# A decode step of attention and an MLP: the output weight loaded in four pieces instead of five, its columns split 320 to 256, and the last wait moved to GpSimd

## The chip, the cores and the metric

The kernel runs on one core of one Trainium2 chip. Its time is device microseconds of one execution, told as a median over several. The page and the views of the profile come from one profiled execution, which has a time of its own.

## What is computed

A batch of four rows, one token each, width 576. The input is normalised once; an attention over the last 2048 places of a cache (32 query heads, 16 heads of K and V) and an MLP block run on it, and the results are added to the input:

```python
def _A_ref(x, k_cache, v_cache, wq, wo):                 # x: 4 x 1 x 576
    q = (x @ wq).reshape(B, Sq, Hq, Dh)...               # 32 heads of 128
    scores = einsum("bhqd,bhkd->bhqk", q, k[last 2048]) * Dh**-0.5
    o = einsum("bhqk,bhkd->bhqd", softmax(scores), v[last 2048])
    return o.reshape(B, Sq, Hq * Dh) @ wo                # wo: 4096 x 576
def _B_ref(x, w1, w2, w3, w4):
    h = gelu(layernorm(x) @ w1)                          # one token: half of its shifted groups are zeros
    x1 = x + shifted(h) @ w2
    return x1 + gelu(layernorm(x1) @ w3) @ w4            # w4: 4608 x 576
xn = layernorm(x)
return x + _A_ref(xn, ...) + _B_ref(xn, ...)
```

All inputs and the output are bf16. The weights and the parts of the caches that are read come to 88.5 MB.

## The kernel before

The program is written engine by engine. Each operation is put on a list of its engine with what it waits for and a key; every list is sorted by key (L613) and issued in that order. Nothing else decides the order of the work.

**The stream of loads.** All loads but that of the input go through SP's queue in the order of their keys: w1, w2, wq, w3, then sixteen chunks of K (2 MB each), eight of V (4 MB each, the last one in two halves), w4 and wo. A load waits until the buffer it overwrites has been read: the chunks of K for the transposes of an earlier chunk, those of V for the products of an earlier chunk. w4 (L273) waits until the sixth chunk of V has been used; wo comes behind it in the queue, in pieces (L295 to L299).

**The middle.** TensorE transposes K in blocks of 128 (L485), VectorE and ScalarE copy the blocks out (L469, L468), TensorE takes the scores (L492); softmax, a transposition of the probabilities (L514, L520), then the products with V (L553) while the chunks of V land. A fold (L559, L571 to L577) brings the two heads of a group apart, and three more steps (L580 to L583) make ORT, the attention's output, with the 4096 inner values laid over 128 partitions and 32 rows.

**The end.** The output has 4 rows of 576 columns. It is added up in two accumulators of 288 columns each (`ACC`, L161), which lie in different 32-row groups of the accumulation memory. `pe_t1` (L585) puts input plus MLP residual into them, `pe_MO` (L455) adds w4's product, 36 rows of 128 inner values, two matmuls a row, one for each half of the columns; then wo's product follows, 32 rows, again two matmuls a row (L596 to L607). Ahead of w4's product stand eight matmuls on zeros (`pe_idle`, L592). wo is cut by `WO_ROWS` (L20) into pieces of 13, 10, 5, 3 and 1 rows, each a load with a semaphore of its own; the product of a piece waits for its piece alone. A row of wo is 128 partitions of 576 values, 144 KB. Every piece waits on SP for the same uses of V as before the change, and all of them stand behind w4.

In the last piece the half of columns 288 to 575 goes first (`for h in (1, 0)`, with a smaller key for it). When a half's last matmul is done, VectorE copies columns 288 to 575 (L609) and ScalarE columns 0 to 287 (L608) into `out_sb`. The output's load to memory is issued by ScalarE when both are done (L300), and SP waits for it to land (L301); this is the last instruction of the program.

The lines that the prediction's steps touch: L20, L161, L199 (where every load is issued), L273, L295 to L301, L392 (the helper `acc_mm`, where w4's and wo's matmuls are recorded), L449 and L526 (other evictions), L460, L553, L588, L592, L596 to L609.

Of the kernel before, what the change touches and what calls it, by code (L numbers as in the profile page):

```python
# [7 lines left out]
ACTF = mybir.ActivationFunctionType  # L8
# [8 lines left out]
NVS = 4  # L17
NPAIR = 2
ACT_EVAC = (1, 4, 7)
WO_ROWS = (13, 10, 5, 3, 1)  # L20
WOA = 28
V_IDLE = 4
O_IDLE = 8
# [14 lines left out]
def bass_parallel_sum__sliding_block_cached__mixer_s_mlp__decode_kernel(  # L38
    nc, A_x, A_k_cache, A_v_cache, A_wq, A_wo, B_x, B_w1, B_w2, B_w3, B_w4, out
):  # L40
    B, Sq, D = A_x.shape
# [14 lines left out]
    scale = float(Dh) ** -0.5  # L56
    EPS = 1e-5
    HALF = D // 2
    FH = F // 2
    W4R = F // 128  # L60
    CH = [(b, gq) for gq in range(4) for b in range(B)]
# [8 lines left out]
    with ExitStack() as ctx:  # L70
        def sb(name, shape, dt):
            return ctx.enter_context(nc.sbuf_tensor(name, shape, dt))
# [16 lines left out]
        wq_t = kring[:, 2 * UE:2 * UE + 9 * NQ // 2]  # L89
        w3_t = vring[:, 0:9 * FH]  # L90
        w4_t = vring[:, 5 * UE - W4R * D:5 * UE].rearrange("p (r n) -> p r n", r=W4R)
        assert 9 * FH <= 4 * UE
        assert WOA * D <= 2 * UE and (32 - WOA) * D + W4R * D <= 3 * UE
        wo_at = lambda a: a * D if a < WOA else 2 * UE + (a - WOA) * D
        wot = lambda a, n: vring[:, wo_at(a):wo_at(a) + n * D].rearrange("p (r n) -> p r n", r=n)
        _o = 0

        def cut(n):
            nonlocal _o
            _o += n  # L100
            return ktb[:, _o - n:_o]
        w1_t = cut(9 * HALF)
        w2_t = cut(9 * HALF)
        assert _o <= NKT // 2 * 1024
# [18 lines left out]
        hs_inT = sb("hs_inT", [128, 9, 2, B], BF16)  # L123
        hh_sb = sb("hh_sb", [2 * B, HALF], BF16)
        h2_sb = sb("h2_sb", [128, 64 * 9], BF16)
        q_sb = vring[:, 5 * UE - 512:5 * UE]
        h2T_sb = sb("h2T_sb", [128, W4R, B], BF16)
# [6 lines left out]
        ident_f = sb("ident_f", [128, 128], FP32)  # L134
# [16 lines left out]
        ORT = sb("ORT", [128, 32, B], BF16)  # L151
        t1 = sb("t1", [B, D], FP32)
        out_sb = sb("out_sb", [B, D], BF16)

        ps = ctx.enter_context(nc.psum_tensor("ps", [128, 8, 512], FP32))[:]
# [2 lines left out]
        OTps = ps[:, 1, 0:2 * NX]  # L158
        rinvps = ps[:, 5, 0:128]
        ORps = ps[:, 2, 0:128]  # L160
        ACC = [ps[32 * k:32 * k + B, 7, 0:HALF] for k in range(2)]  # L161
        Qps = ps[:, 4, :]
        QTps = ps[:, 0, 0:256].bitcast(BF16).rearrange("p (n j x) -> p n j x", n=4, j=4)
        HSps = ps[0:B, 5, 0:HALF]
        HHps = ps[0:2 * B, 3, 0:HALF]
        TS = ((0, 5), (5, 4))
# [4 lines left out]
        S = {}  # L171
# [16 lines left out]
        def add(engine, emit, waits=(), sig=None, key=0.0, inc=None):  # L188
            seqc[0] += 1
            prog[engine].append(Op(emit, waits, sig, key, seqc[0], inc))  # L190

        def add_dma(pairs, skey, waits=(), key=0.0, engine="sp"):
            if skey not in S:
                S[skey] = sem("s_" + "_".join(str(k) for k in (skey if isinstance(skey, tuple) else (skey,))))
            dma_count[skey] = dma_count.get(skey, 0) + 16 * len(pairs)

            def emit(e):
                for o_, i_ in pairs:
                    e.dma_start(o_, i_).then_inc(S[skey], 16)  # L199
            add(engine, emit, waits, None, key)  # L200
            return ("dma", skey, dma_count[skey])
# [21 lines left out]
        KE = KV + 40.0  # L223
# [26 lines left out]
        for gl in range(2):  # L250
            for x in range(2 * NVS):
# [3 lines left out]
                  waits=["pick11"], sig=f"pick2{gl}{x}", key=-84 + 0.1 * (8 * gl + x))  # L255


        def mask_of(t, tag, view):
            add("dve", lambda e: e.tensor_reduce(out=t[:], in_=view, axis=AX.X, op=ALU.add), waits=["ident_f"], sig=tag, key=-8)
        add("dve", lambda e: e.tensor_reduce(out=par[:], in_=ident_f[:].rearrange("p (m a) -> p a m", a=2), axis=AX.X, op=ALU.add),  # L260
            waits=["ident_f"], sig="par", key=-29.5)
# [32 lines left out]
        ev_wo, WOR, a = [], [], 0  # L294
        for n, rc in enumerate(WO_ROWS):  # L295
            ev_wo.append(add_dma([(wot(a, rc), wos[:, a:a + rc, :])], ("wo", n), [f"PV{2 * (NCV - NVS + (a >= WOA)) + 1}"], KS + NC + n))
# [1 line left out]
            a += rc  # L298
        assert a == 32  # L299
        ev_o = add_dma([(o2, out_sb[:])], "out", ["fin1", "fin0"], 10000, engine="act")  # L300
        add("sp", lambda e: e.wait_ge(S[ev_o[1]], ev_o[2]), (), None, 10001)  # L301


        def ln_ops(idx, src, dst, first_waits, tag, k0):
# [79 lines left out]
        for k in range(2):  # L384
            for g in range(2):
                add("dve", lambda e, k=k, g=g: e.tensor_copy(
                        out=qp_out[:, :, 2 * k + g].rearrange("p b (j n) y -> p b j n y", j=2),
                        in_=QTps[:, :, 2 * g:2 * g + 2, B * k:B * (k + 1)].rearrange("p (n y) j b -> p b j n y", y=2)),
                    waits=["qTp"] + (["qpad_zero"] if k + g == 0 else []), sig=f"qT{2 * k + g}", key=-10 + 0.1 * k)

        def acc_mm(e, h, lhsT, rhs, start=False, stop=False):
            return e.matmul(ACC[h], lhsT=lhsT, rhs=rhs, start=start, stop=stop, tile_position=(0, 32 * h), skip_group_check=True)  # L392

# [14 lines left out]
        for h in range(2):  # L408
# [3 lines left out]
                waits=[f"hs{h}"], sig="x1" if h else "x1a", key=-27 + 0.1 * h)  # L412
# [3 lines left out]
            waits=["hT", "ln3_sd"], sig="gelu_h", key=-25.9)  # L416
# [5 lines left out]
        def pe_h2(k):  # L422
            t0, n = TS[k]

            def f(e):
                ins = None
                for s_ in range(9):
                    w = w3_t[:, FH * s_:FH * (s_ + 1)].rearrange("x (p t) -> x p t", t=W4R)
                    for j in range(4):
# [17 lines left out]
        for k in range(2):  # L447
            add("pe", pe_h2(k), waits=[ev_w3] + (["xs20", "xs21", "gelu_h", "h2_zero"] if k == 0 else []), sig=f"h2_{k}", key=-18 + k)
            add("act", lambda e, k=k: e.activation(out=h2_v[k], in_=H2ps[k], func=ACTF.Gelu_apprx_tanh), waits=[f"h2_{k}"],  # L449
                sig=f"gelu2_{k}", key=-5 + 0.1 * k)  # L450
# [4 lines left out]
        def pe_MO(t0, t1):  # L455
            def f(e):
                ins = None
                for t in range(t0, t1):
                    for h in range(2):
                        ins = acc_mm(e, h, h2T_sb[:, t, :], w4_t[:, t, HALF * h:HALF * (h + 1)])  # L460
                return ins
            return f
        add("pe", lambda e: e.wait_ge(S["pool"], resolve("perm_bf")[1]), waits=["qT3"], key=-1)
# [2 lines left out]
        def evac(n):  # L466
            if n % 8 in ACT_EVAC:
                return "act", lambda e: e.activation(out=ktbuf[:, n % NKT], in_=tb[n % 4], func=ACTF.Copy)  # L468
            return "dve", lambda e: e.tensor_copy(out=ktbuf[:, n % NKT], in_=tb[n % 4])  # L469

        for n in range(NB):
            c, k = n // NBLK, n % NBLK
            if k == 0:
                add("dve", lambda e, c=c: e.tensor_copy(out=Qs[:, c % N_CB, :], in_=Qpad_t[:, 128 * (4 * CH[c][0] + CH[c][1]):][:, 0:128]),
                    waits=[f"SC{c - 2}"] if c >= 1 else ["qT3"], key=n)
            eng, f = evac(n)
            w = [f"T{n}"] + ([f"SC{c - 2}"] if c >= 1 else [])
            add(eng, f, waits=w + (["hT", "hs1", "h2_1"] if n == 0 else []), key=n + 0.2, inc=(("E", n % LB), 1))
# [9 lines left out]
        def emit_SC(e, k):  # L488
# [11 lines left out]
            waits=["rmax"], sig="negb", key=KS + 0.05)  # L500
        for q in range(4):
            add("act", lambda e, q=q: e.activation(out=P_sb[:, q, :], in_=Sps[:, q, :], func=ACTF.Exp,
                                                   bias=negb[:, 0:1], scale=scale, accum_out=rs4[:, q:q + 1]),
                waits=["negb"], sig=f"exp{q}", key=KS + 0.1 + 0.01 * q)
# [16 lines left out]
        for qt in range(4):  # L521
            k0 = KS + 0.9 + 0.1 * qt
            add("pe2", pe_PT(qt), waits=[f"PTx{q}" for q in range(4)] + (["pick217"] + [f"E{NB - 1 - k}" for k in range(4)] if qt == 0 else []),
                sig=f"PTp{qt}", key=k0)
            if qt % 2 == 1:
                add("dve", lambda e, qt=qt: e.tensor_copy(out=PT_t[:, 512 * qt:512 * (qt + 1)], in_=ps[:, 4 + qt, :]),  # L526
                    waits=[f"PTp{qt}"], sig=f"PT{qt}", key=k0)
            else:
                add("act", lambda e, qt=qt: e.activation(out=PT_t[:, 512 * qt:512 * (qt + 1)], in_=ps[:, 4 + qt, :], func=ACTF.Copy),
                    waits=[f"PTp{qt}"], sig=f"PT{qt}", key=k0)  # L530
# [3 lines left out]
            waits=["rinv", "ident_f"], sig="diag", key=KS + 0.82)  # L534
        add("pe2", lambda e: e.matmul(rinvps, lhsT=ones_f[:], rhs=diag[:], start=True, stop=True),
            waits=["diag", "ones_f", "PT1"], sig="rinvp", key=KV + 0.5)
        add("dve", lambda e: e.tensor_copy(out=rinvB[:].rearrange("p (c u e) -> p c u e", u=NU, e=2),
                                           in_=rinvps.rearrange("p (u c e) -> p c u e", u=NU, e=2)),
            waits=["rinvp"], sig="rinvB", key=KV - 2)
# [29 lines left out]
        for bp in range(NPAIR):  # L569
            k0 = KV + 2 * NVS * (bp + 1) - 0.5  # L570
            add("dve", lambda e: e.tensor_scalar(out=tmp[:], in0=ps[:, 0, 128:256], scalar1=maskd[:, 1:2], scalar2=None, op0=ALU.mult),  # L571
                waits=[f"PV{2 * NVS * (bp + 1) - 1}", "maskd"], sig=f"F{bp}", key=k0)
# [4 lines left out]
                waits=["rinvB", f"fold{bp}"], sig=f"O{bp}", key=k0 + (3 if bp == 0 else 0.2))  # L577
# [5 lines left out]
            waits=["OR"], sig="ORT", key=KE + 0.3)  # L583

        def pe_t1(e):  # L585
            ins = None
            for h in range(2):
                ins = e.matmul(ACC[h], lhsT=ident_f[0:B, 0:B], rhs=t1[:, HALF * h:HALF * (h + 1)], start=True, stop=False,  # L588
                               tile_position=(0, 32 * h), skip_group_check=True)
            return ins  # L590
        add("pe3", pe_t1, waits=["t1", "ident_f", "PT3"], sig="t1in", key=KE - 4)
        add("pe3", pe_idle(O_IDLE), key=KE + 0.25)  # L592

        add("pe3", pe_MO(0, W4R), waits=[ev_w4, "h2T"], key=KE + 10)
        last_p = len(WOR) - 1
        for n, (r0, r1) in enumerate(WOR):  # L596
            def f(e, r0=r0, r1=r1, hs=(0, 1)):
                ins = None
                for r in range(r0, r1):
                    for h in hs:  # L600
                        ins = acc_mm(e, h, ORT[:, r, :], wot(r, 1)[:, 0, HALF * h:HALF * (h + 1)], stop=(r == 31))
                return ins
            if n < last_p:
                add("pe3", f, waits=[ev_wo[n], "ORT"], sig=f"AO{n}", key=KE + 20 + n)
            else:
                for h in (1, 0):
                    add("pe3", lambda e, f=f, h=h: f(e, hs=(h,)), waits=[ev_wo[n]], sig=f"AOl{h}", key=KE + 20 + n - 0.1 * h)  # L607
        add("act", lambda e: e.activation(out=out_sb[:, 0:HALF], in_=ACC[0], func=ACTF.Copy), waits=["AOl0"], sig="fin0", key=KE + 50)  # L608
        add("dve", lambda e: e.tensor_copy(out=out_sb[:, HALF:D], in_=ACC[1]), waits=["AOl1"], sig="fin1", key=KE + 50)  # L609


        for eng in prog:
# [38 lines left out]
        e = nc.tensor  # L651
        emit_program("pe", "pe", e)
        with nc.Fori(0, N_LOOP, engines=[PE]) as it:
# [7 lines left out]
            for j in range(LB):  # L661
                emit_T(e, j, wait)
                if j % NBLK == 2:
                    k = (j // NBLK - 1) % N_CB
# [53 lines left out]
```

## Time and profile before

| | us |
|---|---|
| median of 3 runs | 214.08 (213.81 to 214.11) |
| the profiled execution | 213.93 |
| its span, first to last instruction | 212.6 |
| mean granted TensorE clock in it | 0.928 |
| PE busy in it (81% of the span) | 172.5 |
| DVE busy in it (53%) | 111.9 |
| ACT busy in it (28%) | 58.6 |
| bytes loaded, and their mean rate | 88.49 MB, 416 GB/s |
| the share of SP's queue of the 16 DMA engines' time | 97.7% |

The engines' names in the profile: PE is the matmul side of TensorE and PEld its loading of weights, DVE is VectorE, ACT is ScalarE, POOL is GpSimd, and SPq or ACTq is the issuing side of an engine. In the row of slices each digit is a fortieth of the span in tenths of busy time; PEclk is the granted TensorE clock, in tenths of full speed. In the timeline a row gives start, length, engine, line, operation, what it writes and reads, the count of instructions that were merged into it and, in brackets, how long the engine had been idle ahead of it and what released it. A matmul's end is modelled, and matmuls overlap, so a merged row's length is from its first start to its last end.

### The profile page before, as it was taken

Reading aid. Unit: us, or ns where it says so; the run is one execution under the profiler, and the core shown is the slowest. Engines: PE = TensorE matmul, PEld = TensorE weight load, DVE = VectorE, ACT = ScalarE, POOL = GpSimd, SP = SyncE. Lnnn points to the kernel's source line nnn. Section 1 sums busy time; section 2 is a strip of 40 time slices with the busy share of each in tenths; the row PEclk is TensorE's granted clock in tenths of the full one; section 3 lists DMA queues with packets and bytes.
Section 4 is the critical chain, followed back from the end, with each engine's and each line's share of the span. In section 5 each row is a group of like instructions: output and inputs, shape, how many; then the busy total and the mean of one; then the engine's idle time right before and its main releaser. Section 6 shows DMA issues by size and latency. Waiting matters only on the chain.

```text
span 212.6 us, 4856 instructions
## 1 busy us (share of the span) xinstructions
PE 172.5 (81%) x2212; PEld 133.7 (63%) x2216; DVE 111.9 (53%) x168; ACT 58.6 (28%) x69; POOL 15.6 (7%) x38
## 2 busy tenths in 40 slices
PE   1456147999999999999996089999989598997495
PEld 0222014888878888887774048988868487883262
DVE  5433200477776777777764869995575444003000
ACT  2004001366665566666656520000000000000000
POOL 8991000000000000000000000000000000000000
PEclk9997855899999999999999589999999889999799
DMA  6999999999999999999999999999999999999993
GB/s 242 453 444 445 429 396 416 432 425 427 429 416 438 432 422 429 435 422 424 432 444 438 444 407 459 413 425 453 407 444 438 419 425 410 451 476 393 407 408 131
DMA packets 5066, 88.65 MB, mean 417 GB/s; under 512 B 568, under 2 KB 704, under 8 KB 1216
## 3 DMA queue, kind: packets, MB, share of 16 engines
q1 hardware_dynamic: 5040, 88.49, 97.7%
q8 instruction: 8, 0.13, 0.3%
q14 instruction: 2, 0.02, 0.0%
q10 hardware_dynamic: 16, 0.01, 0.0%
HBM read 88.49 MB, written 0.00 MB: 416 GB/s over the span
## 4 chain that ended last, share of the span: by engine, by line
DMA 47%; PE 45%; DVE 4%; SPq 1%; ACT 1%; issue 1%
PE ps L485 23%; DMA vring<-in_A_wo_dram 15%; DMA vring<-in_B_w_dram 13%; DMA vring<-in_A_v_cache_dram 12%; PE ps L553 11%; DMA kring<-in_A_k_cache_dram 7%; PE ps L492 6%; PE ps L430 2%; SPq L199 1%; DVE vring L520 1%; DVE rmax L498 1%; DVE ktb L545 1%; PE ps L514 1%; PE ps L347 1%; ACT ktb L468 0%
## 5 line engine op out<-in xcount | busy, mean ns | idle before, releaser
L469 DVE COPY ktb<-ps 128x1024 bf16<-128x1024 bf16 x80 | 53.8, 689 | 23.5 <-PE ps L485 23.4
L485 PEld LDWEIGHTS ps<-perm_bf,kring 128*128 128x128 bf16 x1024 | 58.2, 98 | 8.3 <-issue 7.6
L485 PE MATMUL ps<-perm_bf,kring 128*128 128x128 bf16 x1024 | 61.7, 220 | 0.2
L468 ACT ACTIVATE ktb<-ps 128x1024 bf16<-128x1024 bf16 x48 | 48.0, 1023 | 32.5 <-PE ps L485 32.1
L545 DVE TENSOR_TENSOR ktb<-kring,mH_bf 128x4096 bf16<-128x4096 bf16 x16 | 36.2, 2286 | 14.6 <-PE ps L553 14.6
L553 PE MATMUL ps<-vring,ktb 128*128 128x256 bf16 x256 | 30.3, 282 | 4.3 <-DMA vring<-in_A_v_cache_dram 3.5
L553 PEld LDWEIGHTS ps<-vring,ktb 128*128 128x128 bf16 x256 | 25.7, 101 | 8.5 <-issue 3.6
L553 PE MATMUL ps<-kring,ktb 128*128 128x256 bf16 x256 | 28.6, 273 | 0.9 <-DMA kring<-in_A_v_cache_dram 0.9
L553 PEld LDWEIGHTS ps<-kring,ktb 128*128 128x128 bf16 x256 | 25.0, 98 | 4.5 <-issue 1.1
L608 ACT ACTIVATE out_sb<-ps 4x288 bf16<-4x288 f32 x1 | 0.4, 399 | 84.6 <-PE ps L392 84.6
L492 PE MATMUL ps<-ktb,Qs 128*32 128x512 bf16 x272 | 17.8, 382 | 1.2 <-ACT ktb L468 1.2
L430 PE MATMUL ps<-vring,xs 128*8 128x320 bf16 (+1 forms) x72 | 4.5, 429 | 7.6 <-DMA vring<-in_B_w_dram 7.6
L492 PEld LDWEIGHTS ps<-ktb,Qs 128*32 128x32 bf16 x272 | 5.7, 96 | 6.7 <-DVE ktb L469 1.4
L514 PE MATMUL ps<-vring,pick_bf 128*32 128x256 bf16 x64 | 3.9, 411 | 6.4 <-DVE rinv L532 6.4
L609 DVE CAST out_sb<-ps 4x288 bf16<-4x288 f32 x1 | 0.4, 449 | 15.7 <-PE ps L392 15.7
L392 PE MATMUL ps<-vring,h2T_sb 128*4 128x288 bf16 x72 | 6.2, 347 | 3.1 <-DMA vring<-in_B_w_dram 3.1
L571 DVE TENSOR_SCALAR tmp<-ps,maskd 128x128 f32<-128x128 f32 x2 | 0.7, 350 | 14.8 <-PE ps L553 14.8
L430 PEld LDWEIGHTS ps<-vring,xs 128*8 128x8 bf16 x72 | 2.1, 110 | 9.8 <-DMA vring<-in_B_w_dram 8.0
L330 PE MATMUL ps<-ident_bf,xp_bf 4*128 4x4 bf16 x15 | 0.8, 163 | 8.1 <-DVE xp_bf L314 5.0
L392 PEld LDWEIGHTS ps<-vring,h2T_sb 128*4 128x4 bf16 x72 | 3.7, 101 | 5.8 <-DMA vring<-in_B_w_dram 3.6
L514 PEld LDWEIGHTS ps<-vring,pick_bf 128*32 128x32 bf16 x64 | 2.0, 118 | 8.2 <-DVE rinv L532 6.9
L239 POOL MEMSET ktb<- 128x8192 bf16 x1 | 6.9, 6924 | 0.0
(93 smaller groups left out, 78.6 us busy)
## 6 DMA issues: line engine op xcount, KB each, us to landing
kring<-in_A_k_cache_dram SPq DMA_DIRECT2D x16, 2048.0 KB, 13.8
vring<-in_A_v_cache_dram SPq DMA_DIRECT2D x4, 4096.0 KB, 24.6
kring<-in_A_v_cache_dram SPq DMA_DIRECT2D x3, 4096.0 KB, 34.0
vring<-in_B_w_dram SPq DMA_DIRECT2D x2, 5184.0 KB, 25.1
kring<-in_A_wq_dram SPq DMA_DIRECT2D x1, 4608.0 KB, 15.7
kring<-in_A_v_cache_dram SPq DMA_DIRECT2D x2, 2048.0 KB, 27.4
vring<-in_A_wo_dram SPq DMA_DIRECT2D x1, 1872.0 KB, 26.9
vring<-in_A_wo_dram SPq DMA_DIRECT2D x1, 1440.0 KB, 29.8
```

The costliest lines, as they stand in the source:

```text
L199: e.dma_start(o_, i_).then_inc(S[skey], 16)
L239: P(lambda e: e.memset(ktb[:, NKT // 2 * 1024:NKT * 1024], 0.0), key=-92, inc=(("E", LB - 2), 1))
L347: ins = e.matmul(ps[:, w, :], lhsT=zeros_bf[:, 0:128], rhs=zeros_bf[:, :], start=True, stop=True)
L392: return e.matmul(ACC[h], lhsT=lhsT, rhs=rhs, start=start, stop=stop, tile_position=(0, 32 * h), skip_group_check=True)
L430: ins = e.matmul(H2ps[k][32 * j:32 * j + 2 * B].rearrange("b (p t) -> b p t", t=n), lhsT=x_at(2, s_), rhs=w[:, :, 9 * j + t0:9 * j + t0 + ...
L468: return "act", lambda e: e.activation(out=ktbuf[:, n % NKT], in_=tb[n % 4], func=ACTF.Copy)
L469: return "dve", lambda e: e.tensor_copy(out=ktbuf[:, n % NKT], in_=tb[n % 4])
L485: ins = e.transpose(tb[j % 4][:, t, :], kslot_t(k)[:, 8 * kb + t, :], perm_bf[:])
L492: ins = e.matmul(Sps[32 * u:32 * u + 32, q, :].rearrange("p (t i) -> p t i", t=16), lhsT=Qs[:, k, 32 * u:32 * u + 32], rhs=ktgrp[:, (4 * k ...
L514: ins = e.matmul(ps[32 * j:32 * j + 32, 4 + qt, 256 * ih:256 * (ih + 1)].rearrange("p (t a e) -> p t a e", a=NPAIR, e=2), lhsT=pick_bf[:, ...
L545: return lambda e: e.tensor_tensor(out=PTpad[:, n % 4], in0=PTv[:, qt, NH * h:NH * (h + 1), bp, :].unsqueeze(2).to_broadcast([128, NH, NX, ...
L553: ins = e.matmul(ps[:, 0, 0:256], lhsT=PTpad[:, 2 * (k % 2) + h, 2 * g:2 * g + 2].rearrange("p t h e -> p (t h e)"), rhs=vslot(k)[:, Dh * ...
```

## The change

Three things at once, all in the kernel's end. wo is cut into four pieces of 20, 8, 3 and 1 rows. The 576 columns are cut at 320 instead of 288, so the first accumulator takes columns 0 to 319 and the second 320 to 575, in every matmul that goes into them (`pe_t1`, w4, wo) and in the two copies; in the last piece the first half now goes first. The wait for the output's landing is put on GpSimd instead of SP.

```diff
-WO_ROWS = (13, 10, 5, 3, 1)
+WO_ROWS = (20, 8, 3, 1)
...
+    OC = (0, 320, D)
...
-        ACC = [ps[32 * k:32 * k + B, 7, 0:HALF] for k in range(2)]
+        ACC = [ps[32 * k:32 * k + B, 7, 0:OC[k + 1] - OC[k]] for k in range(2)]
...
-        add("sp", lambda e: e.wait_ge(S[ev_o[1]], ev_o[2]), (), None, 10001)
+        add("pool", lambda e: e.wait_ge(S[ev_o[1]], ev_o[2]), (), None, 10001)
...
-                        ins = acc_mm(e, h, h2T_sb[:, t, :], w4_t[:, t, HALF * h:HALF * (h + 1)])
+                        ins = acc_mm(e, h, h2T_sb[:, t, :], w4_t[:, t, OC[h]:OC[h + 1]])
...
-                ins = e.matmul(ACC[h], lhsT=ident_f[0:B, 0:B], rhs=t1[:, HALF * h:HALF * (h + 1)], start=True, stop=False,
+                ins = e.matmul(ACC[h], lhsT=ident_f[0:B, 0:B], rhs=t1[:, OC[h]:OC[h + 1]], start=True, stop=False,
...
-                        ins = acc_mm(e, h, ORT[:, r, :], wot(r, 1)[:, 0, HALF * h:HALF * (h + 1)], stop=(r == 31))
+                        ins = acc_mm(e, h, ORT[:, r, :], wot(r, 1)[:, 0, OC[h]:OC[h + 1]], stop=(r == 31))
...
-                for h in (1, 0):
-                    add("pe3", lambda e, f=f, h=h: f(e, hs=(h,)), waits=[ev_wo[n]], sig=f"AOl{h}", key=KE + 20 + n - 0.1 * h)
-        add("act", lambda e: e.activation(out=out_sb[:, 0:HALF], in_=ACC[0], func=ACTF.Copy), waits=["AOl0"], sig="fin0", key=KE + 50)
-        add("dve", lambda e: e.tensor_copy(out=out_sb[:, HALF:D], in_=ACC[1]), waits=["AOl1"], sig="fin1", key=KE + 50)
+                for h in (0, 1):
+                    add("pe3", lambda e, f=f, h=h: f(e, hs=(h,)), waits=[ev_wo[n]], sig=f"AOl{h}", key=KE + 20 + n - 0.1 * (1 - h))
+        add("act", lambda e: e.activation(out=out_sb[:, 0:OC[1]], in_=ACC[0], func=ACTF.Copy), waits=["AOl0"], sig="fin0", key=KE + 50)
+        add("dve", lambda e: e.tensor_copy(out=out_sb[:, OC[1]:D], in_=ACC[1]), waits=["AOl1"], sig="fin1", key=KE + 50)
```

The number of matmuls, of bytes and of copies is the same; there is one load fewer.

## The prediction, as it went on record

> **What bounds the kernel now.** I read the page's slices first, then the chain of work that ended last in order of time, then the DMA issues, and then the timeline of the last 14 us.
>
> ```profile
> span 212.6 us, 4856 instructions
> POOL 8991000000000000000000000000000000000000
> PEclk9997855899999999999999589999999889999799
> DMA  6999999999999999999999999999999999999993
> ```
>
> One digit stands for 5.3 us. The DMA engines are at nine tenths or more from the second slice to the last but one: nearly the whole run is one unbroken stream of loads through SP's queue, and only its beginning and its end are free. The change touches nothing of the stream before wo, so the question is what happens behind the last bytes.
>
> ```profile
> 176.55 0.33 SPq L199
> 176.88 0.04 issue
> 176.92 0.43 SPq L199
> ...
> 178.35 31.68 DMA vring<-in_A_wo_dram
> ...
> 210.07 0.70 PE ps L392 x8
> 210.78 0.44 DVE out_sb L609
> ```
>
> This is the end of the chain (start, length, what). SP issues w4 at 176.55 and behind it the five wo pieces 0.48 us apart (0.43 each, then the next after 0.04). The fourth lands 31.68 us behind its issue, at 210.03, eight matmuls run, then the eviction. Each piece's landing follows from its issue and its time to landing:
>
> ```profile
> vring<-in_A_wo_dram SPq DMA_DIRECT2D x1, 1872.0 KB, 26.9
> vring<-in_A_wo_dram SPq DMA_DIRECT2D x1, 1440.0 KB, 29.8
> ...
> vring<-in_A_wo_dram SPq DMA_DIRECT2D x1, 720.0 KB, 31.1
> vring<-in_A_wo_dram SPq DMA_DIRECT2D x1, 432.0 KB, 31.7
> vring<-in_A_wo_dram SPq DMA_DIRECT2D x1, 144.0 KB, 31.6
> ```
>
> Issues at 176.92, 177.40, 177.87, 178.35 and 178.83 give landings at 203.8, 207.2, 209.0, 210.05 and 210.4. The pieces were issued some 27 us before they land, so they stand in the queue behind V and w4, and their landings are set by bytes, not by SP.
>
> ```profile
> 199.40 6.20 PE L392 MATMUL ps<-vring,h2T_sb 128*4 128x288 bf16 x72 [3.10 <-DMA vring<-in_B_w_dram]
> 205.31 1.56 PEld L392 LDWEIGHTS ps<-vring,ORT 128*4 128x4 bf16 x26
> 207.26 1.07 PEld L392 LDWEIGHTS ps<-vring,ORT 128*4 128x4 bf16 x20 [0.40 <-DMA vring<-in_A_wo_dram]
> 209.00 0.46 PEld L392 LDWEIGHTS ps<-vring,ORT 128*4 128x4 bf16 x10 [0.67 <-DMA vring<-in_A_wo_dram]
> 210.07 0.43 PEld L392 LDWEIGHTS ps<-vring,ORT 128*4 128x4 bf16 x8 [0.62 <-DMA vring<-in_A_wo_dram]
> 210.42 0.08 PEld L392 LDWEIGHTS ps<-vring,ORT 128*4 128x4 bf16 x2
> 210.76 0.45 DVE L609 CAST out_sb<-ps 4x288 bf16<-4x288 f32 x1 [15.72 <-PE ps L392]
> 210.80 0.40 ACT L608 ACTIVATE out_sb<-ps 4x288 bf16<-4x288 f32 x1 [84.57 <-PE ps L392]
> 211.28 0.28 ACTq L199 DMA_DIRECT2D out_dram<-out_sb  x1
> ```
>
> The weight loads show when each piece can begin, 0.04 us behind its landing: so the landings are 207.22, 208.96, 210.03 and, for the last row, 210.38. In every gap PE waits for bytes. The last row alone decides: its load at 210.42, DVE at 210.76, output DMA issued at 211.28, span over at 212.6.
>
> The profiled execution took 213.93 us, its span 212.6, so 1.3 us lie around the span. The median of the runs is 214.08 (213.81 to 214.11): 0.15 above this execution, which lies inside their spread.
>
> **The change, part by part.**
>
> *wo in four pieces.* No byte is saved. By the landings above, 10 rows took 3.4 us (203.8 to 207.2), 5 took 1.74, 3 took 1.07: about 0.34 a row and 0.05 to 0.08 a piece. One piece fewer brings the later landings forward by 0.08 at most: estimates 208.9 for row 27, 209.95 for row 30 and 210.30 for row 31. SP's saved issue (0.48) buys nothing, because the pieces wait behind 27 us of other bytes. But rows 0 to 12 no longer come at 203.8: rows 0 to 19 come together at 203.8 + 7 x 0.34 = 206.2. What hides that wait is w4's product, which keeps PE until 205.3 now. PE then has 32 rows left at 206.2, where before it had done 13 by about 207 and then waited.
>
> *320 to 256 columns.* What does a row cost PE? From the chain, the timeline, the busy time by stretches and the groups by line, in this order:
>
> ```profile
> 135.06 7.00 PE ps L553 x64
> 205.43 1.76 PE L392 MATMUL ps<-vring,ORT 128*4 128x288 bf16 x26
> 199.40:202.70 3.30, 3.30 (x28) 1.81 (x30) 0.00 (x0) 0.00 (x0) 0.00 (x0) 0.50 0.98 419
> L392 PE MATMUL ps<-vring,ORT 128*4 128x288 bf16 x8 | 0.7, 285 | 0.3 <-DMA vring<-in_A_wo_dram 0.3
> ```
>
> 64 matmuls of 256 columns in V's product take 7.00 us, 0.109 each, or 2.34 columns a ns. The 26 matmuls of 13 rows take 1.76 from the first start to the last end; less one duration of 0.285 that is 12 steps of 0.123. That is 288 columns at 2.34 a ns: a row's two halves run side by side, and the wider one sets the pace. So a row will cost 0.123 x 320/288 = 0.1365, not the same sum of 576 columns. (The Trainium skill, "TensorEngine Tiling (Array Packing)", Key Properties, says that tiles operate independently and different ones can execute in parallel; the trace's 0.123 agrees. If the halves went one behind the other, the split would cost nothing, and the sum would be ruled by the landings, 0.08 earlier.)
>
> w4's 36 rows would take 36 x 0.123 = 4.4 us; they took 6.0 (199.40 to wo's first matmul at 205.43), because the granted clock is 0.50 in the stretch from 199.40 to 202.70 (its row: us, busy time of PE, PEld, DVE, ACT and POOL, granted clock, DMA share, GB/s). So 1.6 us are lost to the clock. With the same loss the new 36 rows take 36 x 0.1365 + 1.6 = 6.5: PE is through at 205.9. That is still ahead of the 206.2 at which rows 0 to 19 land, so this 0.5 us is hidden, with 0.3 to spare.
>
> Then from 206.21 on PE has work without a gap: rows 20 to 27 are there (208.9) before it has done 20 rows (208.94), rows 28 to 30 (209.95) before row 28 is due (210.03). Row 31 begins at 206.21 + 31 x 0.1365 = 210.44, where the landing would allow 210.34 and before it was 210.42: **+0.02**. So PE becomes the bound of the last 4 us, by 0.1, and eats the 0.08 that the saved piece gives.
>
> *The evictions.* Prices by width, from the groups by line:
>
> ```profile
> L449 ACT ACTIVATE h_sb<-ps 128x320 bf16<-128x320 f32 x1 | 0.4, 437 | 11.2 <-PE ps L430 11.2
> L526 DVE CAST kring<-ps 128x512 bf16<-128x512 f32 x2 | 1.4, 686 | 1.8 <-PE ps L514 1.8
> L609 DVE CAST out_sb<-ps 4x288 bf16<-4x288 f32 x1 | 0.4, 449 | 15.7 <-PE ps L392 15.7
> ```
>
> ACT: 0.437 for 320 columns of 128 partitions, 0.40 for 288 of four (the timeline above), so 0.43 for 320 of four. DVE: (686-449)/224 = 1.06 ns a column, so 256 take 0.415. Now DVE ends last (211.21) and ACT at 211.20: they are balanced. After, the 320-column half ends 0.014 later (32 columns at 2.34), ACT starts at 210.83 and ends at 211.26; DVE is through at about 211.18. The output DMA follows the later one; with the same 0.07 it is issued at 211.33: **+0.05 in all** (the +0.02 is in it). The order of the halves is right for ACT (its half goes first) but the two start within 0.04 of each other, so it is worth no more than that.
>
> *GpSimd awaits the landing.* Nothing is queued behind the wait on GpSimd, whose work ends in the page's fourth slice, before 22 us, and nothing behind SP's either. The rows are of the waits and the timeline's start:
>
> ```profile
> SPq L301 <- DMA out_dram<-out_sb: 33.3, 1, 33.3
> 0.80 0.52 POOL L232 MEMSET zeros_bf<- 128x512 bf16 x1 [0.29 <-POOLq L703]
> 0.80 0.85 SPq L199 DMA_DIRECT2D ktb<-in_B_w_dram  x2
> ```
>
> SP's wait is the last instruction of the span. No row shows GpSimd waiting for a DMA at the end. The nearest: at the start both engines pass the same barrier and do their first work at 0.80, so the wake-up differs by some 0.01. What comes behind the span on each engine no row shows; it is bounded by the whole start of a program up to that first work, 0.8 us, either way. I take 0, the nearest row, and keep both ends as a doubt. (The Trainium skill, "Runtime: NRT & Kernel Launch", The ~15µs preamble/postamble breakdown, puts the hop of the barrier between engines at 44 ns, eight of them; another engine being last would move it by a few hops, an estimate of 0.1 to 0.2 us by that page, of unknown sign. No run here shows it.)
>
> **Sum:** 213.93 + 0.05 = 213.98 on the profiled execution, 214.13 on the median; I say **214.05**, midway between the two.
>
> **The rivals.**
>
> *Ruled by landings (same).* If the landings come later than I interpolate, or the halves are not bound to each other, row 31 stands at 210.34 instead of 210.44: 213.85. Inside the same class.
>
> *The end is cheaper with GpSimd last (faster).* If what follows SP's wait outside the span is longer than what follows GpSimd's, up to 0.8 us goes: 213.2 to 213.6, 213.4 as its middle. For it: 1.3 us lie outside the span, and no row shows what they are. Against it: the start shows both engines alike. From 0.45 us on it decides the class. The same unknown with the other sign gives 214.6.
>
> *PE at half clock in the wo rows (slower).*
>
> ```profile
> 165.20:168.61 3.41, 0.94 (x10) 0.84 (x10) 2.33 (x2) 0.00 (x0) 0.00 (x0) 1.00 1.03 442
> 192.51:195.92 3.41, 2.44 (x14) 1.06 (x11) 1.62 (x5) 0.00 (x0) 0.00 (x0) 1.00 1.06 455
> 195.92:199.33 3.41, 0.38 (x2) 0.00 (x0) 0.00 (x0) 0.00 (x0) 0.00 (x0) 1.00 0.80 337
> ```
>
> After a stretch of 3.4 us with PE busy 0.38 us the granted clock was 0.50 (the window from 199.40 above); one with 2.44 us did no harm. If the slow stretch doesn't fall on w4's product, PE is through with it at 199.40 + 36 x 0.1365 = 204.3 and idles until 206.2. 1.9 us of idling in 3.4 leave 1.5 us busy, between the two rows. Should that be taken for idling, 3.4 us of wo rows run at half clock and 1.7 us are lost with no gap left to take it up: 215.7. Before, the gaps of 0.4, 0.67 and 0.62 took up most of such a loss. Against it: it needs a stretch that begins elsewhere than in the profiled run, in most of the runs.
>
> *The change does not do what it says.* Four wo issues, the widths and the waiting engine stand in the program as written; nothing else is moved.
>
> **How the numbers follow.** Forecast with the landings rival, within 0.43 us (0.2%, about what a measurement of this kernel can tell from no change): 0.62. Faster end: 0.22. Slower: 0.16, of which 0.06 for the half clock and 0.10 for a costlier end. The likeliest case alone is 213.8 to 214.3. The range must leave out no more than 2 in 10, so it takes in the end's unknown cost but for its far ends, and leaves out the half clock: 213.4 to 214.6.
>
> **What would show it.** Four wo landings at about 206.2, 208.9, 209.95 and 210.3; w4's matmuls until about 205.9; wo's weight loads without a gap from 206.2; row 31 at 210.44; DVE's eviction shorter than ACT's; output DMA at 211.33; the span 212.65 and 1.3 us around it. Wrong would be: gaps in wo's weight loads (then the pace isn't 0.1365), half clock behind 206, or a time around the span that is not 1.3.

## The result, and the profile after

The changed kernel takes 214.73 us (median of 11 runs, 214.33 to 215.52), the kernel before 213.91 in the runs beside it (213.70 to 214.11): a ratio of 1.0038 (95% interval 1.0030 to 1.0046). It is slower by 0.8 us, where the sum had 0.05. One of all the executions told of below, with the last wait on VectorE, took 354.22 us with 1.32 us around its span, and is left out of that kernel's figures.

First, where the loss lies: inside the span, or around it (the device time less the span). The profiled execution of the changed kernel took 214.75 us at a span of 212.9, so 1.85 us lie around the span; before it was 213.93 and 212.6, so 1.33. Over all 11 runs the time around the span is 1.85 (1.75 to 1.93). So 0.5 to 0.6 us of the 0.8 stand in no row of an instruction: they came behind or ahead of all that the profile's views show. The rest is inside.

The chain of waits that ended last, from its tail (start, length, what):

```profile
175.44 30.94 DMA vring<-in_A_wo_dram
206.38 0.04 issue
206.43 4.63 PE ps L393 x54
211.06 0.02 issue
211.08 0.42 DVE out_sb L610
```

Before, the chain came from the fourth piece's landing, and TensorE had only 0.70 us in it. Now it comes from the first piece's landing at 206.38, and TensorE has the 4.6 us from there to the end. The pieces' issues (KB, us to landing):

```profile
vring<-in_A_wo_dram SPq DMA_DIRECT2D x1, 2880.0 KB, 30.9
...
vring<-in_A_wo_dram SPq DMA_DIRECT2D x1, 1152.0 KB, 33.3
vring<-in_A_wo_dram SPq DMA_DIRECT2D x1, 432.0 KB, 33.8
vring<-in_A_wo_dram SPq DMA_DIRECT2D x1, 144.0 KB, 33.7
```

And the timeline of the end:

```profile
199.57 6.73 PE L393 MATMUL ps<-vring,h2T_sb 128*4 128x320 bf16 x72 [3.08 <-DMA vring<-in_B_w_dram]
206.43 2.53 PEld L393 LDWEIGHTS ps<-vring,ORT 128*4 128x4 bf16 x40 [0.47 <-DMA vring<-in_A_wo_dram]
206.43 4.58 PE L393 MATMUL ps<-vring,ORT 128*4 128x320 bf16 x64
209.22 1.48 PEld L393 LDWEIGHTS ps<-vring,ORT 128*4 128x4 bf16 x24 [0.26 <-DMA vring<-in_A_wo_dram]
210.62 0.08 PEld L393 LDWEIGHTS ps<-vring,ORT 128*4 128x4 bf16 x2
211.05 0.43 ACT L609 ACTIVATE out_sb<-ps 4x320 bf16<-4x320 f32 x1 [84.70 <-PE ps L393]
211.08 0.42 DVE L610 CAST out_sb<-ps 4x256 bf16<-4x256 f32 x1 [15.84 <-PE ps L393]
211.56 0.28 ACTq L200 DMA_DIRECT2D out_dram<-out_sb  x1
```

All 64 matmuls of wo stand in one row; before there were three gaps. One short wait is left, too short to part the row: by the trace's records the wide half's matmuls start 0.136 us apart, but row 20 starts 0.211 behind row 19, at 209.22, 0.04 behind the second piece's landing at 209.18. The weight loads show it as the 0.26 ahead of 209.22, longer because the narrow half had run ahead. The last row's weights are loaded at 210.62 and the output is issued at 211.56: 0.94 us from one to the other, where it was 0.86 (210.42 to 211.28). The whole stream came 0.2 us later in this execution (w4's product begins at 199.57 instead of 199.40). That is no work of the change: in the fourteen profiled executions, those of the experiments included, w4 lands between 199.33 and 200.09.

The program's last instruction, by its line:

```profile
L302 POOLq EVENT_SEMAPHORE  x1: 17/17/17, 212.9 to 212.9; - x1
```

It is GpSimd's wait now. It shows 17 ns, and so did SP's before (L301). What GpSimd costs is not in that row.

### The profile page after: what moved, and what is told of

It reads as the page before. It is cut to its first block, busy times and chain, and to the rows that moved or that the text cites. A ratio compares the mean times of both kernels' runs of the same rounds, so it can differ in the third digit from the quotient of the medians.

```text
span 212.9 us, 4859 instructions
## 1 busy us (share of the span) xinstructions
PE 171.4 (81%) x2216; PEld 132.7 (62%) x2216; DVE 112.1 (53%) x168; ACT 59.4 (28%) x69; POOL 15.7 (7%) x38
## 4 chain that ended last, share of the span: by engine, by line
DMA 60%; PE 32%; DVE 4%; ACT 1%; SPq 1%; issue 1%
DMA kring<-in_A_k_cache_dram 21%; DMA vring<-in_A_wo_dram 15%; DMA vring<-in_B_w_dram 13%; PE ps L486 12%; DMA vring<-in_A_v_cache_dram 12%; PE ps L554 10%; PE ps L493 4%; PE ps L393 2%; PE ps L431 2%; DVE vring L521 1%; DVE rmax L499 1%; DVE ktb L546 1%; SPq L200 1%; PE ps L515 1%; PE ps L348 0%
## 5 line engine op out<-in xcount | busy, mean ns | idle before, releaser
L486 PEld LDWEIGHTS ps<-perm_bf,kring 128*128 128x128 bf16 x1024 | 57.4, 98 | 9.5 <-issue 7.4
L469 ACT ACTIVATE ktb<-ps 128x1024 bf16<-128x1024 bf16 x48 | 48.7, 1024 | 31.7 <-PE ps L486 31.0
L554 PE MATMUL ps<-vring,ktb 128*128 128x256 bf16 x256 | 28.6, 273 | 4.4 <-DMA vring<-in_A_v_cache_dram 3.6
L554 PEld LDWEIGHTS ps<-vring,ktb 128*128 128x128 bf16 x256 | 24.8, 98 | 7.7 <-issue 3.6
L393 PE MATMUL ps<-vring,h2T_sb 128*4 128x256 bf16 (+1 forms) x72 | 6.7, 342 | 3.1 <-DMA vring<-in_B_w_dram 3.1
```

Of the source, the lines that this page charges most:

```text
L486: ins = e.transpose(tb[j % 4][:, t, :], kslot_t(k)[:, 8 * kb + t, :], perm_bf[:])
L554: ins = e.matmul(ps[:, 0, 0:256], lhsT=PTpad[:, 2 * (k % 2) + h, 2 * g:2 * g + 2].rearrange("p t h e -> p (t h e)"), rhs=vslot(k)[:, Dh * ...
```

## The experiments

Theory A: what follows the last instruction is longer when GpSimd is the last engine. Theory B, the rival: TensorE's late finish is the whole loss, and the time around the span varies by program. All runs are on one core, each beside runs of the kernel before on the same chip.

**The last wait alone on GpSimd**, with five pieces and halves of 288:

```diff
-        add("sp", lambda e: e.wait_ge(S[ev_o[1]], ev_o[2]), (), None, 10001)
+        add("pool", lambda e: e.wait_ge(S[ev_o[1]], ev_o[2]), (), None, 10001)
```

> The kernel before with the last wait alone moved to GpSimd. Theory A (what follows the last wait costs more on GpSimd than on SP): span as before, 212.6, and about 1.84 us around it instead of 1.33, so some 0.5 us over before. Theory B (the whole loss is TensorE's late finish in the span, and what lies around the span varies from program to program): 0.1 at most over before.

Measured: 214.46 us, ratio 1.0022 (1.0013 to 1.0031). The spans are before's (212.6, against 212.7), and 1.83 us lie around them (1.74 to 1.93) instead of 1.26 (1.20 to 1.39 in 33 runs of before). Its profiled execution shows an end as quick as ever, here the last instruction by its line:

```profile
L301 POOLq EVENT_SEMAPHORE  x1: 17/17/17, 212.4 to 212.4; - x1
```

The span of this execution is 212.4, shorter than before's 212.6; it took 214.21 all the same, where before's took 213.93. Theory A holds: 0.57 us, all of it outside the span.

**The changed kernel with the wait back on SP:**

```diff
-        add("pool", lambda e: e.wait_ge(S[ev_o[1]], ev_o[2]), (), None, 10001)
+        add("sp", lambda e: e.wait_ge(S[ev_o[1]], ev_o[2]), (), None, 10001)
```

> The changed kernel with the last wait back on SP. Theory A: 1.3 us around the span, 0.2 to 0.3 over before, which is the share of pieces and columns. Theory B: 0.8 over before, as the changed kernel.

Measured: 214.13 us, ratio 1.0006 (0.9997 to 1.0015), 1.26 around the span. Without GpSimd the rest of the change can't be told from no change. Theory B falls.

**The pieces alone:**

```diff
-WO_ROWS = (13, 10, 5, 3, 1)
+WO_ROWS = (20, 8, 3, 1)
```

> The kernel before with wo in pieces of 20, 8, 3 and 1 rows, and nothing else. If the wider half sets TensorE's pace, 288 columns do 31 rows in 31 x 0.1225 = 3.8 us from about 206.2, through at 210.0, before the last row lands: the landing decides again, and the time is before's or 0.1 under it. If joining the first two pieces is itself the cost (TensorE idles until 206.2), 0.2 to 0.3 over before.

Measured: 214.11 us, ratio 1.0005 (0.9996 to 1.0014): no difference that the runs can tell. Lines of its timeline:

```profile
206.38 2.62 PE L392 MATMUL ps<-vring,ORT 128*4 128x288 bf16 x40 [0.74 <-DMA vring<-in_A_wo_dram]
209.18 1.68 PE L392 MATMUL ps<-vring,ORT 128*4 128x288 bf16 x24 [0.18 <-DMA vring<-in_A_wo_dram]
210.20 0.45 PEld L392 LDWEIGHTS ps<-vring,ORT 128*4 128x4 bf16 x8 [0.20 <-DMA vring<-in_A_wo_dram]
```

With 288 columns TensorE keeps up: it waits ahead of the 20, the 8 and the 3 rows, and the landing decides.

**The columns alone**, five pieces, SP waiting; the diff is the changed kernel's but for `WO_ROWS` and the wait:

```diff
+    OC = (0, 320, D)
...
-                for h in (1, 0):
+                for h in (0, 1):
```

> The kernel before with the columns cut at 320 and the first half first in the last piece, five pieces, SP waiting. If the pace costs only where it leaves no gap, the gaps ahead of the pieces of 5 and 3 rows take it up: 0.05 over before, from the wider eviction. If 320 columns cost as such, 0.2 to 0.3 over before.

Measured: 213.98 us, ratio 1.0003 (0.9994 to 1.0012). The end of its timeline:

```profile
210.09 0.44 PEld L393 LDWEIGHTS ps<-vring,ORT 128*4 128x4 bf16 x8 [0.48 <-DMA vring<-in_A_wo_dram]
210.84 0.43 ACT L609 ACTIVATE out_sb<-ps 4x320 bf16<-4x320 f32 x1 [84.35 <-PE ps L393]
210.87 0.42 DVE L610 CAST out_sb<-ps 4x256 bf16<-4x256 f32 x1 [15.78 <-PE ps L393]
211.35 0.28 ACTq L200 DMA_DIRECT2D out_dram<-out_sb  x1
```

There is still one gap ahead of the last pieces (0.48 on the weight loads): with 13 rows done early, the wider pace is taken up. Times of this size the runs don't tell; the trace's records do. From the last row's landing to the issue of the output it is 0.90 us before, 0.89 with the pieces alone, 0.94 with the columns alone, 0.98 with both, and 0.89 to 0.91 in the seven executions, e1 and those below, that have before's end with other waits. So the two edits together cost 0.08 inside the span. The last matmul of the last row starts 0.06 us behind the landing before, 0.05 with the pieces alone, 0.09 with the columns alone and 0.14 with both: the columns alone bring out less than half of TensorE's delay, the pieces alone none.

Now the end itself. **Both wait**, SP and GpSimd, for the same landing:

```diff
         add("sp", lambda e: e.wait_ge(S[ev_o[1]], ev_o[2]), (), None, 10001)
+        add("pool", lambda e: e.wait_ge(S[ev_o[1]], ev_o[2]), (), None, 10001)
```

> The kernel before with SP's wait kept and a second wait for the same landing on GpSimd. If GpSimd's own way out of the program is the longer one: around the span 1.83 as in e1, 0.5 over before. If the loss comes from SP leaving early (it ends while the loads still run): 1.26 around the span, before's time.

Measured: 214.74 us in 5 runs, ratio 1.0035 (1.0022 to 1.0049), 1.77 around the span (1.75 to 1.92). That SP leaves early is not the harm; that GpSimd is late is.

**The wait on VectorE, on ScalarE, on TensorE**: the same one line with `"dve"`, `"act"` and TensorE's last list.

> The last wait alone on VectorE. If SP is the cheapest engine to be last, or all but GpSimd are alike, 1.26 or more around the span, before's time or over it; if a hop from engine to engine is what counts, a value between 1.1 and 1.8.

> The last wait alone on ScalarE, which also issues the output. The same question as for VectorE: 1.26 around the span if only GpSimd differs, another value if each engine has its own way out.

> The last wait alone on TensorE. The same question: 1.26 around the span if only GpSimd differs, another value if each engine has its own way out.

| the last engine | kernel | around the span, median (from to), us | ratio to before (95%) |
|---|---|---|---|
| SP | before, beside these three | 1.29 (1.22 to 1.43) | |
| VectorE | e6 | 1.36 (1.32 to 1.48) | 1.0012 (1.0003 to 1.0021) |
| ScalarE | e7 | 1.44 (1.36 to 1.51) | 1.0005 (0.9996 to 1.0014) |
| TensorE | e8 | 1.59 (1.51 to 1.64) | 1.0017 (1.0008 to 1.0026) |
| GpSimd | e1 | 1.83 (1.74 to 1.93) | 1.0022 (1.0013 to 1.0031) |
| GpSimd, with SP | e5 | 1.77 (1.75 to 1.92) | 1.0035 (1.0022 to 1.0049) |

The ratios carry the spans' own scatter; the time around the span is the cleaner reading. It scatters too: the other programs in which SP is last have medians of 1.22 (e3) to 1.35 (e4), so these times alone don't tell VectorE's 1.36 from SP's.

The traces also record every update of a semaphore, a counter on which engines wait for each other, and these records settle where the time lies. One semaphore, number 2, is waited for and updated by no instruction that the profile shows. At the end of every execution it has 18 updates, in two groups of nine, and between the groups some 240 other semaphores have one update each. The table tells what of the first group comes behind the last instruction (the row of SP is of seven profiled executions, alike within 0.01; that of GpSimd of four):

| the last engine | updates of the first group that are left | the first of them, us behind the last instruction | the last of them, us |
|---|---|---|---|
| SP | 5 | 0.13 | 0.29 |
| VectorE | 6 | 0.15 | 0.39 |
| ScalarE | 8 | 0.11 | 0.43 |
| TensorE | 9 | 0.19 | 0.55 |
| GpSimd (e1, e5, e10, changed) | 7 | 0.54 | 0.83 |

From there to the last update of the second group it is 1.14 to 1.15 us in nine executions and 1.23 to 1.25 in five, and both occur with SP and with GpSimd last: that is scatter, not the engine. The whole time around the span is the time to that last update less 0.18 to 0.19 in thirteen of the fourteen executions (less 0.09 in e4's). So the difference between the engines lies behind the last instruction: 0.10, 0.14, 0.26 and 0.54 us over SP. The counts fit a chain that the engines pass in the order TensorE, ScalarE, GpSimd, VectorE, SP and back; that order is inferred, since the records do not name who makes an update. By it GpSimd pays 0.41 more than SP before its own update, and 0.12 for the two updates more that follow it. Why its first one takes 0.54, no trace here shows.

**GpSimd late, but not last.** SP keeps its wait, and GpSimd waits for VectorE's eviction:

```diff
         add("sp", lambda e: e.wait_ge(S[ev_o[1]], ev_o[2]), (), None, 10001)
+        add("pool", lambda e: e.wait_ge(*resolve("fin1")), (), None, 10001)
```

> The kernel before with SP's wait kept, and GpSimd waiting for VectorE's eviction, about 1.35 us ahead of SP's last instruction. If GpSimd's way out runs by itself behind its own last instruction (0.57 longer than SP's), it is through before SP's: 1.26 around the span and before's time. If any late instruction on GpSimd makes the end longer: 1.83 around the span, 0.5 over before.

Measured: 214.20 us, ratio 1.0004 (0.9995 to 1.0013), 1.34 around the span (1.23 to 1.40). 0.5 us did not come: an engine's way out runs beside the others' work, and GpSimd's 0.57 is hidden when its last instruction lies 1.3 us ahead of SP's (211.64 and 212.96 by the trace's records). The third update of the first group, GpSimd's by the order above, comes at 212.34, 0.04 behind the second, as it does in before: nothing waited for it.

**GpSimd awake.** The last wait on GpSimd, which writes a spare tile first:

```diff
+        spare = sb("spare", [128, 1], FP32)
...
+        add("pool", lambda e: e.memset(spare[:], 0.0), ["fin1"], None, 10000)
-        add("sp", lambda e: e.wait_ge(S[ev_o[1]], ev_o[2]), (), None, 10001)
+        add("pool", lambda e: e.wait_ge(S[ev_o[1]], ev_o[2]), (), None, 10001)
```

> The last wait on GpSimd as in e1, but GpSimd writes a spare tile of 128 values when VectorE's eviction is done, 1.35 us ahead of the landing. If its long way out comes from having slept since 17 us: near 1.3 around the span. If it is a property of the engine: 1.83 again, 0.5 over before.

Measured: 214.55 us in 9 runs, ratio 1.0025 (1.0015 to 1.0035), 1.85 around the span (1.75 to 1.92). The timeline shows it awake after 195 us of rest:

```profile
211.46 0.10 POOL L302 MEMSET spare<- 128x1 f32 x1 [194.77 <-DVE out_sb L611]
211.47 0.28 ACTq L200 DMA_DIRECT2D out_dram<-out_sb  x1
```

The long rest is not the cause: awake, GpSimd has its first update 0.54 us behind its last instruction as well.

**Two looks at the order of the evictions**, each one execution. First the kernel before with its first half ahead in the last row:

```diff
-                for h in (1, 0):
-                    add("pe3", lambda e, f=f, h=h: f(e, hs=(h,)), waits=[ev_wo[n]], sig=f"AOl{h}", key=KE + 20 + n - 0.1 * h)
+                for h in (0, 1):
+                    add("pe3", lambda e, f=f, h=h: f(e, hs=(h,)), waits=[ev_wo[n]], sig=f"AOl{h}", key=KE + 20 + n - 0.1 * (1 - h))
```

> The kernel before with the first half ahead of the second in the last row, widths of 288. If the second eviction starts 0.034 behind the first whichever engine it is (both wait for counts of one TensorE semaphore, in order): ScalarE starts about 0.375 behind the last landing, VectorE 0.41, VectorE ends at 0.86 and the output is issued at 0.92 to 0.93 instead of 0.90. If each starts with its own half: no change from 0.90.

```profile
210.82 0.40 ACT L608 ACTIVATE out_sb<-ps 4x288 bf16<-4x288 f32 x1 [84.31 <-PE ps L392]
210.86 0.45 DVE L609 CAST out_sb<-ps 4x288 bf16<-4x288 f32 x1 [15.72 <-PE ps L392]
211.34 0.28 ACTq L199 DMA_DIRECT2D out_dram<-out_sb  x1
```

It took 214.00 us. The starts came as expected, the second 0.04 behind the first, now with VectorE as the second. The issue did not: it is 0.89 behind the last landing, not 0.92 to 0.93. Then the changed kernel with SP waiting and its narrow half ahead:

```diff
-        add("pool", lambda e: e.wait_ge(S[ev_o[1]], ev_o[2]), (), None, 10001)
+        add("sp", lambda e: e.wait_ge(S[ev_o[1]], ev_o[2]), (), None, 10001)
...
-                for h in (0, 1):
-                    add("pe3", lambda e, f=f, h=h: f(e, hs=(h,)), waits=[ev_wo[n]], sig=f"AOl{h}", key=KE + 20 + n - 0.1 * (1 - h))
+                for h in (1, 0):
+                    add("pe3", lambda e, f=f, h=h: f(e, hs=(h,)), waits=[ev_wo[n]], sig=f"AOl{h}", key=KE + 20 + n - 0.1 * h)
```

> The changed kernel with SP waiting and the second half (256 columns) ahead of the first in the last row. By the counts in order VectorE starts as soon as the narrow half is through and ScalarE 0.034 or more behind it, when the wide half is: output issued 0.93 to 0.98 behind the last landing (0.98 in e2). If the late wide half is what counts, ScalarE starts no earlier than 0.47 and the issue stays at 0.96 to 0.98.

```profile
210.77 0.42 DVE L610 CAST out_sb<-ps 4x256 bf16<-4x256 f32 x1 [14.35 <-PE ps L393]
210.87 0.43 ACT L609 ACTIVATE out_sb<-ps 4x320 bf16<-4x320 f32 x1 [84.50 <-PE ps L393]
211.38 0.28 ACTq L200 DMA_DIRECT2D out_dram<-out_sb  x1
```

It took 213.94 us. The issue stands 0.99 behind the last landing, and ScalarE starts 0.47 behind it: the late wide half is what counts. VectorE is through early and it helps nothing. In these rows the output is issued 0.08 us behind ScalarE's end (211.30 to 211.38); so it is in the changed kernel (211.48 to 211.56), and in before, where ScalarE ends at 211.20 and the issue is at 211.28. With the first half ahead at equal widths ScalarE ends at 211.22, VectorE at 211.31, and the issue is at 211.34, close behind VectorE. So the issue is bound by ScalarE's end and some 0.08 (0.085 in thirteen of the fourteen profiled executions), or by VectorE's and some 0.03 (this one execution), whichever is later: the wider half had been given to the engine whose end counts more.

## Why the prediction was wrong, point by point

**The step that failed** is the price of the last wait: "What comes behind the span on each engine no row shows; it is bounded by the whole start of a program up to that first work, 0.8 us, either way. I take 0, the nearest row". It is 0.57 us (1.83 against 1.26 around the span, e1), seven tenths of the 0.8 that was lost. The semaphore records put it behind the last instruction: 0.54 in the profiled executions. The nearest row was the wrong one: that two engines wake alike at the start says nothing on what each does after its last instruction. The wake-up itself was rightly taken as nothing: the trace's records show GpSimd's last instruction 0.024 us behind the landing, SP's 0.016. The 0.8 us of a program's start, taken as a bound on either side, held the value by luck, since no row ties the end to the start; the rival with the cost on this side was given a chance of 0.10 all the same, and the range stopped at 214.6, 0.13 short. What the sentence on the Trainium skill gave (page "Runtime: NRT & Kernel Launch", section "The ~15µs preamble/postamble breakdown": hops of 44 ns, so 0.1 to 0.2 us by estimate) is too small by the runs: between SP and TensorE lie 0.3, between SP and GpSimd 0.57. In the traces the first group's updates follow one another by 0.02 to 0.10 us behind the late engine's own; what the estimate lacked is the 0.54 ahead of GpSimd's first.

**The pace of a row** was right. 64 matmuls of wo took 4.58 us from 206.43; less the last one's 0.30, over 31 rows, that is 0.138 a row, against 0.1365, and without the wait ahead of row 20 it is 0.136. The narrow half started at its own 0.109 a row, came 0.4 us ahead in fifteen rows, and only then went on at 0.136. So the wider half sets the pace. That the halves run beside each other agrees with the Trainium skill ("TensorEngine Tiling (Array Packing)", Key Properties), by which different tiles can execute in parallel.

**TensorE becoming the bound** was right in size, partly by luck. The last row's weights were loaded 0.04 behind its landing, as always; but by the trace's records one of its two matmuls began 0.14 behind the landing instead of 0.06, the wide half's stream being still busy. Expected was a tenth, from a last landing 0.08 earlier and work without a gap from the first piece's landing. Neither came: against before, the 0.075 lost ahead of row 20 is the whole of it. The second piece landed 9.65 us behind w4 instead of 9.55 (208.9), so rows 20 to 27 were not there when TensorE had done 20 rows; from their landing, eleven steps of 0.136 lead to the last matmul. This is one of the gaps in wo's weight loads that the prediction had named as a sign of being wrong, though not because of the pace.

**What w4's product hides** was right: its 36 rows took 6.56 us (the last wide matmul starts at 206.00, and a step is 0.136) where 6.5 was forecast, so in a stream 0.2 us later it was through at 206.1. The first piece landed at 206.38, 6.85 us behind w4, so the wait for 20 rows had its cover.

**The saved piece** was wrong in a small term: no 0.08 came. The last row lands 11.03 us behind w4 before, and 10.88 to 11.04 in all the executions with five pieces; it is 11.04 in the changed kernel and in e3, 11.05 in e2: the piece that went freed nothing at the end.

**The evictions** have the forecast lengths (0.43 and 0.42), but VectorE did not end first: it starts behind ScalarE, since it waits for a later count of the same semaphore, although its own half's last matmul had ended 0.19 earlier. In e12, with its count first, it starts 0.07 behind that matmul. The issue does not follow the later end by 0.07, as the sum had it, but ScalarE's by 0.085. ScalarE starts 0.05 later behind the landing than before and takes 0.03 longer: +0.08 from landing to issue, where the sum had +0.13, less 0.08 for an earlier landing. In all the span's terms are about +0.1 instead of +0.05, and 0.1 and 0.57 make 0.67; the measured loss is 0.64 to 0.98 by its interval, and the 0.15 from 0.67 to its middle is not told from the scatter of the spans.

**The rivals.** "The end is cheaper with GpSimd last" had the right place and the wrong sign. "PE at half clock in the wo rows" was not what happened in the profiled execution. Its granted clock by stretches (us; busy PE, PEld, DVE, ACT, POOL; clock, DMA share, GB/s):

```profile
200.50:203.90 3.40, 3.40 (x32) 1.79 (x27) 0.00 (x0) 0.00 (x0) 0.00 (x0) 0.50 0.97 416
206.43:211.00 4.57, 4.57 (x64) 3.08 (x64) 0.00 (x0) 0.00 (x0) 0.00 (x0) 1.00 0.58 227
```

The half clock fell on w4's product again, and wo ran at full clock. What this rival feared as its condition came in e12's execution: w4's product ran at full clock and was through at 204.43, TensorE waited 1.80 us for the first piece, and wo's 64 matmuls from 206.23 on still had a granted clock of 1.00. So that much idling did no harm there, in the one execution that shows it. Whether the one run at 215.52, with a span of 213.6, was such a case stays open: it has no trace. Before has one much like it in 33 runs (214.72, with a span of 213.5).

## What to carry to other kernels

The time around the span belongs to the sum: when an edit changes which engine does the last instruction, price that by a run of that edit alone, and leave the last wait to SP if nothing speaks against it. Here an engine with a long way out cost nothing when it was done 1.3 us earlier; nothing between that and 0 was tried. Where two streams side by side share a loop, the wider set the pace of both here, and that showed only when the gaps that took it up were gone.

## What the runs showed that was not expected

The time around the span goes by the last engine: 1.22 to 1.35 us for SP, 1.36 for VectorE, 1.44 for ScalarE, 1.59 for TensorE, 1.77 to 1.85 for GpSimd. The semaphore records show these differences behind the last instruction.

Half clock can last two stretches. In e9's execution w4's product began at half clock and took 7.4 us instead of 6.2:

```profile
199.78 7.09 PEld L393 LDWEIGHTS ps<-vring,h2T_sb 128*4 128x4 bf16 x72 [3.59 <-DMA vring<-in_B_w_dram]
206.91 3.97 PEld L393 LDWEIGHTS ps<-vring,ORT 128*4 128x4 bf16 x64
```

By the trace's records the clock was at half from 198.79 to 205.62. All of wo's weights were then loaded without a gap, and the output was issued 0.91 us behind the last landing, as ever: at 288 columns and five pieces the gaps ahead of the pieces were the reserve in this execution. What the changed kernel does in one was not tried.

The 16 completions of one load are spread: the last row's 16 come between 1.8 and 2.5 us apart from first to last, in every profiled execution, by the trace's records.
